# Two attention and gated-MLP layer pairs on one core: the up product copied by ScalarE, and the first chunk planned ahead

## The chip, the core and the metric

The kernel runs on one core of a Trainium2 chip. The engines of that core work side by side, each through its own queue in order: TensorE (PE in the profile; PEld is its weight load) multiplies matrices into PSUM, VectorE (DVE) and ScalarE (ACT) do element work between PSUM and SBUF, GpSimd (POOL) does some set-up, and SyncE (SP) issues the DMA transfers. An engine that needs another's result waits on a semaphore, and everything behind the waiting instruction waits with it. The metric is the device time of one execution in microseconds, taken as the median of several.

## The reference

The input x has 2048 tokens of 576 numbers in bfloat16. Four layers follow each other, attention and MLP in turn, and the same weights serve both pairs:

```python
x = x + A(layernorm(x))   # attention
x = x + B(layernorm(x))   # gated MLP
x = x + A(layernorm(x))
x = x + B(layernorm(x))

# A: 32 heads of 18; token s sees the 8 tokens s, s-2, ..., s-14
qkv = x @ wqkv
logits = einsum("bhsd,bhswd->bhsw", q, kg) * scale    # masked before token 0
o = einsum("bhsw,bhswd->bhsd", softmax(logits), vg)
A = o @ wo

# B: F = 4608, no activation function
h = (x @ w_gate) * (x @ w_up)
B = h @ w_down
```

## The kernel before

**Chunks.** The tokens are worked through in 17 pieces called chunks (j = 0 to 16). Each goes through one attention layer and the MLP behind it. The first two chunks have 128 tokens (nst = 1), the other fifteen 256 (nst = 2). The first eight token tiles go through both layer pairs, and then the other eight. All weights of the MLP but w_down stay in SBUF; w_down is read again for every chunk, two blocks of 128 rows at a time, into seven places.

**The MLP.** The 36 blocks of 128 hidden features are made in units of 512 columns in PSUM: 9 units in a chunk of 128 tokens, 18 in one of 256. A unit has one bank for the gate product (pg) and one for the up product (pu). In the wide chunks the contraction is cut in two halves of 64 rows that run side by side in the array (`quarter`, L947): a unit's first half, then that of its neighbour, then the two second halves. Between the halves stands a one-element copy by ScalarE (`fence`, L493), which makes the second half's matmuls wait for the first's. When a unit's products are complete, `evac` (L960) empties it: ScalarE copies the gate product to SBUF as bfloat16 (L964), and VectorE multiplies the up product, read from PSUM, with it (L965). The result h goes to one of six places, and the unit's banks are free when VectorE is done. A third of the units makes a phase (nph = 3); at its end `down` or `down2` multiplies the phase's h with w_down, in the wide chunks also in two halves (L1021, L1022), and VectorE adds the sums to x (L992, L1001).

**Attention.** `head` (L409) normalises: statistics on VectorE (L417, L418, or in halves L421, L423), the inverse deviation on ScalarE (L432, L433), the factor nmr on VectorE (L437), the normalised rows on ScalarE (L443, L445, L448). The transposed rows come from TensorE in the first chunks (L467, L469, copied out at L474, L476, L479), and from DMA transposes later (L460). `project` (L539) multiplies with wqkv (L549), and the copies out of PSUM are L631, L633, L643, L660 and L667. The scores are products of q with shifted k on VectorE (L704, L727), partly summed there (L708 to L713) and summed over the head by TensorE (L719); then come the maximum (L745), the difference (L749), the exponential (L753), the sum (L757) and its reciprocal (L762). The weights must then stand on all partitions of a head: in the first chunks by a matmul called spread (L781) and copies, later by a round trip through DRAM (L791, L794). The eight products with shifted v are L811. They are added up by VectorE (L833), except in the very first chunk, called fast, where TensorE adds them: `gather` (L813) multiplies each with the identity into the same banks (L815, L816), and VectorE divides at the end (L838, L841). In that chunk the eight products alternate between two places in SBUF, prod0 and prod1. The output projection is L855 or L876, its residual sum L846.

**The start.** The columns of wqkv are permuted after loading (`perm`, L347, copies at L358): five row blocks, for each the query, key and value parts of 512 columns and the tails. VectorE and ScalarE share the query and key parts; the value parts, wq2, are all ScalarE's (VP, L24). TensorE runs matmuls without use (L1138) where the plan sees it idle at the start.

**The order of the work.** Nothing is left to chance in the order: every operation is entered into a `Plan` with an engine, a cost in nanoseconds, what it reads and writes, a priority and a rank. The rank is -1 for urgent work (`due=True`: the work of `evac` and `fence`), the chunk's number for attention, 60 for the MLP, 0.5 for the permutations. `Plan.run` takes the operation that could start first by these costs, and emits the instructions in that order. Before it takes an operation of rank over 0, it looks whether the same engine has one of lower rank that would become ready before the first would end: for rank 0 (the first chunk) within GUARD of that end, for urgent work up to SLACK earlier. The order holds for DMA issues too. The semaphores between the engines follow from the data; the plan's times only give the order.

Of the kernel before, what the change touches and what calls it, by code (L numbers as in the profile page):

```python
# [10 lines left out]
ACT = mybir.ActivationFunctionType  # L11
ALU = mybir.AluOpType
# [4 lines left out]
class Op:  # L17
    __slots__ = ("eng", "cost", "fn", "deps", "order", "succ", "n", "prio", "idx", "hold", "free",
                 "lat", "margin", "ready", "end", "nbytes", "use", "pair", "need", "rank", "late", "half")
# [7 lines left out]
IDLE = (2000, 300)  # L27
GUARD = {"DVE": 300, "ACT": 300, "PE": 600, "POOL": 0, "SP": 0}
# [4 lines left out]
class Plan:  # L33
# [13 lines left out]
    def op(self, eng, cost, fn, r=(), w=(), prio=1, after=None, hold=None, free=None, margin=0, nbytes=0, use=None,  # L47
           pair=None, need=None, due=False, late=0, half=False):
        o = Op()
        o.rank, o.late, o.half = -1 if due else self.rank, late, half  # L50
# [32 lines left out]

    def run(self, slots):
        clock = {e: 0.0 for e in self.LAT}
# [5 lines left out]
        while cand:  # L91
            best = None
            urgent = {}
            for o in cand:
                t = 0.0
                for p in o.deps:
                    e = p.ready if p.eng != o.eng else p.end
                    if e > t:
                        t = e
                t += o.margin  # L100
                if o.hold is not None:
                    f = free[o.hold]
                    if not f:
                        continue
                    t = max(t, min(f)[0] + o.margin)
                if o.pair is not None:
                    if len(free["unit"]) < len(o.pair):
                        continue
                    t = max(t, min(free["unit"])[0] + o.margin)
                if o.need is not None:  # L110
                    t = max(t, o.need["at"])
                t = max(t, clock[o.eng])
                key = (t, o.prio, o.idx)
                if best is None or key < best[0]:
                    best = (key, o)
                urgent.setdefault(o.eng, []).append((key, o))
            assert best is not None, "the plan is stuck"
            o = best[1]
            if o.rank > 0:
                end = best[0][0] + o.cost  # L120
                ahead = [(c[1].rank, c[0], c[1]) for c in urgent[o.eng] if c[1].rank < o.rank and c[1].rank < LOOK[o.eng]
                         and c[0][0] < end + GUARD[o.eng] * (c[1].rank == 0) - SLACK[o.eng] * (c[1].rank < 0)
                         and c[0][0] < best[0][0] + IDLE[min(max(c[1].rank, 0), 1)]]
                if ahead:
                    best = min(ahead, key=lambda c: c[:2])[1:]
# [28 lines left out]
            if o.free is not None:  # L154
                u = o.use
                u["last"] = max(u.get("last", 0.0), o.ready)
                u["left"] = u.get("left", 1) - 1
                if u["left"] == 0:
                    free[o.free].append((u["last"], u["slot"]))
            o.fn()  # L160
            done += 1
            for s in o.succ:
                s.n -= 1
                if s.n == 0:
                    cand.append(s)
# [4 lines left out]
def kernel(  # L170
# [162 lines left out]

    def setup_b():
# [11 lines left out]
        for k in range(KT):  # L346
            def perm(eng, cost, key, t3, rk, k=k):  # L347
# [10 lines left out]
                op(eng, cost, lambda: fn(dst, src), r=rk, w=[key], prio=2 + (t3 in (2, 4)))  # L358
# [29 lines left out]
        op("ACT", 0, lambda: None, r=[f"wq{t}_{k}" for t in (2, 4) for k in range(KT)], w=["s11", "s12", "ab"])  # L388
# [20 lines left out]
    def head(src, keys, nst, dst, key, prio, ab, on_pe, mg, c0=0, halves=False, parts="nt", xr=()):  # L409
# [3 lines left out]
        for i in range(nst if "n" in parts else 0):  # L413
# [5 lines left out]
            if halves:  # L419
                for a in range(2):  # L420
                    op("DVE", 400, lambda a=a, i=i: nc.vector.bn_stats(out=st[:, ia + i, a, :], in_=src(i)[:, a * HD:(a + 1) * HD]),  # L421
                       r=[f"{keys[i]}h{a}"], w=[f"st{ab}{ia + i}{a}"], prio=prio)
                op("DVE", 210, lambda i=i: nc.vector.bn_aggr(out=mv[:, ia + i, :], in_=st[:, ia + i]),  # L423
# [91 lines left out]
    def attention(j, la, t0, nst):  # L515
# [23 lines left out]
        def project(tag, au, bu, tl, ea, eb, dkeys):  # L539
# [5 lines left out]
            wk = [f"wq{t}_{k}" for t in tw for k in range(KT)]  # L545
# [41 lines left out]
            elif fast:  # L587
                o = None
                for part in (0, 1):
                    u, parts, ts = (ua, au + bu[4:5], (0, 1, 3)) if part == 0 else (ub, bu[:4] + bu[5:], (2, 4))  # L590
                    key = (ka, kb)[part]
                    for k in range(KT):
                        def fn(k=k, part=part):
# [7 lines left out]
                            else:  # L601
# [4 lines left out]
                               r=xk + [f"wq{t}_{k}" for t in ts], w=[key], prio=0, **kw)  # L606
# [91 lines left out]
        for p_ in range(W // 2):  # L698
# [25 lines left out]
            pk, sk = f"prod{p_ % 2}", f"s1{p_}"  # L724
            if nst == 2:
                for e in range(2):
                    op("DVE", 70 + 2.6 * n, lambda p_=p_, e=e: nc.vector.tensor_tensor(  # L727
                        late["prod"][p_ % 2][:, e, :, 0:n], qT[:, :, 0:n], kT[:, :, HALO - DIL * (2 * p_ + 1 - e):HALO - DIL * (2 * p_ + 1 - e) + n], op=ALU.mult),
                       r=qk, w=[pk], prio=prio)
            else:  # L730
                op("DVE", 70 + 5.2 * n, l1, r=qk, w=[pk], prio=prio)
            if fast:
                kw = b1.take() if p_ == 0 else dict(w=[b1.key])
                op("PE", 20 * 20, lambda p_=p_: esel(p_, lambda: [late["prod"][p_ % 2][:, :, k, :] for k in range(KT)]),
                   r=["sel", pk, "cap", "ident"], prio=0, **kw)
            else:
                op("DVE", 82 + 2.02 * n, l2, r=[pk], w=[pk], prio=prio)
                op("DVE", 276 + 2.02 * n, l3, r=[pk], w=[sk], prio=prio)
# [65 lines left out]
        for i_ in range(W):  # L804
# [3 lines left out]
            def pv(i_=i_, o0=o0, to_o=to_o):  # L808
# [4 lines left out]
            def gather(i_=i_):  # L813
                pr = late["prod"][i_ % 2][:, 0]
                nc.tensor.matmul(bo[0]()[:, 0:KF * n], lhsT=ident[:], rhs=pr[:, 0:KF, 0:n], start=(i_ == 0), stop=(i_ == W - 1))  # L815
                nc.tensor.matmul(bo[1]()[:, 0:n], lhsT=ident[:], rhs=pr[:, KF, 0:n], start=(i_ == 0), stop=(i_ == W - 1))  # L816
            op("DVE", 70 + 2.63 * n, pv, r=vk + abk, w=["oT"] if to_o else [f"prod{i_ % 2}"], prio=prio)
            if fast:
                if i_ == 0:
                    ob0 = op("PE", 0, lambda: None, w=[bo[1].key], prio=0, hold=bo[1].pool, use=bo[1].use)  # L820
                    op("PE", 330, gather, r=["prod0", "ident"], w=[bo[0].key, bo[1].key], prio=0, hold=bo[0].pool, use=bo[0].use)
# [8 lines left out]
                else:  # L830
                    op("PE", 330, gather, r=[f"prod{i_ % 2}", "ident"], w=[bo[0].key, bo[1].key], prio=0)
            elif i_:
                op("DVE", 70 + 2.63 * n, lambda i_=i_: nc.vector.tensor_tensor(oT[:, :, 0:n], oT[:, :, 0:n], late["prod"][i_ % 2][:, 0, :, 0:n],  # L833
                                                                        op=ALU.add), r=[f"prod{i_ % 2}"], w=["oT"], prio=prio)
# [71 lines left out]
    def glu(j, t0, nst, last):  # L906
# [53 lines left out]
        def evac(u):  # L960
# [3 lines left out]
            op("ACT", 490, lambda: nc.scalar.copy(g_sb[gs][:, 0:ul], pg[use["slot"]][:, 0:ul]), r=[f"wg_{j}_{u}"], w=[f"g{gs}"], prio=0, due=True)  # L964
            op("DVE", 605, lambda: nc.vector.tensor_tensor(hb[hs][:, 0:ul], pu[use["slot"]][:, 0:ul], g_sb[gs][:, 0:ul], op=ALU.mult),  # L965
# [158 lines left out]
    for j, (l, t0, nst) in enumerate(seq):  # L1124
# [8 lines left out]
        if j == 0:  # L1133
            op("PE", 0, lambda: None, w=list(pool_keys["boot"]), free="unit", use={"slot": NB - 1})
# [6 lines left out]
    with tc.manual_schedule():  # L1141
        nc.vector.memset(g_sb[1][:], 0.0)
        pl.run({**{k: len(v) for k, v in banks.items()}, "unit": NB - 1})
# [28 lines left out]
```

## Time and profile before

| | |
|---|---|
| median of 3 runs | 1048.43 us (1048.34 to 1051.18) |
| the profiled execution | 1051.13 us, its span 1049.3 us |
| TensorE busy | 1033.9 us, 99% |
| VectorE busy | 783.3 us, 75% |
| ScalarE busy | 409.6 us, 39% |
| GpSimd busy | 8.5 us, 1% |
| HBM | 113 GB/s over the span |
| granted TensorE clock | 1.0 |

A line of a group of instructions gives the line of the code, the engine, the operation, what it writes and reads, shapes and count; then the time in which the group was busy, the mean duration in nanoseconds, and the idle time of the engine just before, with what ended it. Neighbours on an engine overlap a little: two instructions of 586 ns that follow each other take less than twice that. A line of a timeline gives the start, the duration, the engine and the instruction, with "x4" where several were merged. A line of waits names who waited, for whom, the sum in microseconds, how often, and the longest.

### The profile page before, as it was taken

How to read it: one execution, taken by the hardware profiler on the slowest of the kernel's cores; microseconds unless marked ns; L12 is line 12 of the kernel's file. 1: busy time of each engine (PE TensorE's matmuls, PEld its weight loads, DVE VectorE, ACT ScalarE, POOL GpSimd, SP SyncE). 2: the span in 40 equal slices, each digit the busy share in tenths (PEclk: the TensorE clock that was granted, in tenths of full speed). 3: DMA queues.
4: the chain of work that ended last, by engine and by line, in shares of the span. 5: the costliest groups of instructions: out<-in, count | busy, mean ns of one | idle time of the engine just before them, and what ended most of it. 6: DMA issues, size and time to landing. Idle time of an engine off the chain costs nothing.

```text
span 1049.3 us, 40035 instructions
## 1 busy us (share of the span) xinstructions
PE 1033.9 (99%) x17898; PEld 827.8 (79%) x17909; DVE 783.3 (75%) x1446; ACT 409.6 (39%) x1105; POOL 8.5 (1%) x33
## 2 busy tenths in 40 slices
PE   7999999999999999999999999999999999999998
PEld 3888778789798887878887777877887788777776
DVE  7698978898899879797989573675878748833233
ACT  6643533243434553333434223434344252232231
POOL 3000000000000000000000000000000000000000
PEclk9999999999999999999999999999999999999999
DMA  8967333443425433335352625233252334343332
GB/s 253 328 209 217 88 101 110 144 108 94 99 91 134 137 76 125 107 110 164 89 130 76 179 72 132 93 103 95 88 157 82 99 91 127 117 133 98 116 103 70
DMA packets 144541, 129.67 MB, mean 124 GB/s; under 512 B 43440, under 2 KB 143728, under 8 KB 144368
## 3 DMA queue, kind: packets, MB, share of 16 engines
q1 hardware_dynamic: 144368, 127.10, 42.7%
q8 instruction: 140, 2.29, 0.9%
q14 instruction: 33, 0.27, 0.1%
HBM read 114.02 MB, written 4.19 MB: 113 GB/s over the span
## 4 chain that ended last, share of the span: by engine, by line
PE 84%; DVE 10%; DMA 3%; issue 1%; ACT 1%; SPq 1%; DVEq 0%; ACTq 0%
PE pg L953 16%; PE pu L953 16%; PE pu L1021 6%; PE acct L953 6%; PE pa L953 6%; PE pa L1021 5%; PE pg L1021 5%; PE acct L1021 4%; PE pg L549 3%; PE pu L549 3%; DVE scr L811 2%; PE pg L855 2%; DVE oT L833 2%; PE pu L929 2%; PE pg L929 1%; DMA scr<-a_dram 1%
## 5 line engine op out<-in xcount | busy, mean ns | idle before, releaser
L953 PEld LDWEIGHTS <-wg 64*128 64x128 bf16 x4320 | 393.7, 94 | 30.5 <-issue 1.7
L953 PE MATMUL pg<-xnT_B,wg 64*128 64x256 bf16 x3200 | 412.3, 269 | 1.6 <-ACT xnT_B L479 1.1
L953 PEld LDWEIGHTS <-wu 64*128 64x128 bf16 x4320 | 392.4, 94 | 25.7 <-issue 1.7
L953 PE MATMUL pu<-xnT_B,wu 64*128 64x256 bf16 x3200 | 411.4, 269 | 0.1
L1021 PEld LDWEIGHTS <-h 64*128 64x128 bf16 x2112 | 122.6, 94 | 102.5 <-DVE h L965 1.0
L1022 PE MATMUL pg<-wd,h 64*128 64x64 bf16 x1008 | 190.5, 189 | 0.0
L1022 PE MATMUL pu<-wd,h 64*128 64x64 bf16 x1008 | 190.5, 189 | 0.0
L965 DVE TENSOR_TENSOR h<-pu,g_sb 128x512 bf16<-128x512 f32 x218 | 147.1, 686 | 49.8 <-ACT g_sb L964 49.2
L493 ACT COPY tok<-pu 1x1 f32<-1x1 f32 x291 | 42.8, 147 | 322.0 <-PE pu L953 214.0
L964 ACT CAST g_sb<-pg 128x512 bf16<-128x512 f32 x218 | 126.9, 586 | 103.8 <-PE pg L953 85.0
L953 PE MATMUL acct<-xnT_B,wg 64*128 64x256 bf16 x1120 | 152.7, 269 | 0.0
L953 PE MATMUL pa<-xnT_B,wu 64*128 64x256 bf16 x1120 | 152.4, 269 | 0.2
L1021 PE MATMUL pu<-wd,h 64*128 64x512 bf16 x576 | 149.5, 377 | 0.4 <-ACT tok L493 0.3
L1021 PE MATMUL pg<-wd,h 64*128 64x512 bf16 x576 | 149.3, 377 | 0.2 <-DVE h L965 0.2
L1021 PE MATMUL pa<-wd,h 64*128 64x512 bf16 x480 | 123.8, 377 | 0.0
L1021 PE MATMUL acct<-wd,h 64*128 64x512 bf16 x480 | 123.7, 377 | 0.0
L1022 PEld LDWEIGHTS <-h 64*128 64x128 bf16 x2112 | 121.6, 95 | 1.2 <-issue 0.4
L549 PEld LDWEIGHTS <-wqkv 64*128 64x128 bf16 (+1 forms) x2030 | 102.8, 94 | 15.8 <-issue 3.5
L727 DVE TENSOR_TENSOR scr<-qT,kv 128x1280 bf16<-128x1280 bf16 x112 | 88.5, 816 | 25.7 <-ACT kv L633 25.7
L953 PE MATMUL pg<-xnT_B,wgu_t 64*128 64x256 bf16 x400 | 107.6, 269 | 0.0
L953 PE MATMUL pu<-xnT_B,wgu_t 64*128 64x256 bf16 x400 | 107.6, 269 | 0.0
L549 PE MATMUL pg<-xnT_A,wqkv 64*128 64x256 bf16 (+2 forms) x863 | 100.0, 265 | 1.1 <-DVE xf L1001 0.8
(172 smaller groups left out, 1497.3 us busy)
## 6 DMA issues: line engine op xcount, KB each, us to landing
wd<-in_B_w_down_dram SPq DMA_DIRECT2D x306, 288.0 KB, 4.5
scr<-a_dram SPq DMA_DIRECT2D x56, 128.0 KB, 2.7
wg<-in_B_w_gate_dram SPq DMA_DIRECT2D x6, 768.0 KB, 9.5
wu<-in_B_w_up_dram SPq DMA_DIRECT2D x6, 768.0 KB, 11.2
xb<-in_A_x_dram SPq DMA_DIRECT2D x7, 288.0 KB, 2.9
out_dram<-xf SPq DMA_DIRECT2D x14, 144.0 KB, 3.3
a_dram<-scr SPq DMA_DIRECT2D x14, 128.0 KB, 2.0
scr<-in_A_wqkv_dram SPq DMA_DIRECT2D x4, 288.0 KB, 5.2
```

The costliest lines, as they stand in the source:

```text
L493: box["at"] = nc.scalar.copy(tok[0:1, :], src())
L549: return nc.tensor.matmul(bank(p_, u)[0:m, e * n:(e + 1) * n], lhsT=wqkv[r_, k, w0:w0 + m], rhs=xnT_A[r_, k, c0:c0 + n], start=start, stop ...
L727: op("DVE", 70 + 2.6 * n, lambda p_=p_, e=e: nc.vector.tensor_tensor(late["prod"][p_ % 2][:, e, :, 0:n], qT[:, :, 0:n], kT[:, :, HALO - DI ...
L811: nc.vector.tensor_tensor(js(dst), js(vT[:, :, o0:o0 + n]), abw, op=ALU.mult)
L833: op("DVE", 70 + 2.63 * n, lambda i_=i_: nc.vector.tensor_tensor(oT[:, :, 0:n], oT[:, :, 0:n], late["prod"][i_ % 2][:, 0, :, 0:n], op=ALU. ...
L855: return nc.tensor.matmul(bank(hh, us[i])[:, 0:HD], lhsT=oT[rows, t, i * P:(i + 1) * P], rhs=wo_p[rows, t, hh * HD:(hh + 1) * HD], start=( ...
L929: nc.tensor.matmul(pt[:, e * n:(e + 1) * n], lhsT=w_[:, k, ft * P:(ft + 1) * P], rhs=xT[:, k, 0:n], start=(first and k == 0 and e == 0), s ...
L953: return nc.tensor.matmul(ps[:, e * n:(e + 1) * n], lhsT=w_, rhs=xT[rows, k, 0:n], start=(first and e == 0 and k == 0), stop=(not first an ...
L964: op("ACT", 490, lambda: nc.scalar.copy(g_sb[gs][:, 0:ul], pg[use["slot"]][:, 0:ul]), r=[f"wg_{j}_{u}"], w=[f"g{gs}"], prio=0, due=True)
L965: op("DVE", 605, lambda: nc.vector.tensor_tensor(hb[hs][:, 0:ul], pu[use["slot"]][:, 0:ul], g_sb[gs][:, 0:ul], op=ALU.mult), r=[f"wu_{j}_{ ...
L1021: return [lambda: nc.tensor.matmul((pg, pu)[i][use["slot"]][:], lhsT=lhs, rhs=wt[rows, e % 2, 0:512], start=first, stop=fin, skip_group_ch ...
L1022: lambda: nc.tensor.matmul((pg, pu)[i][tl["slot"]][:, 0:TL], lhsT=lhs, rhs=wt[rows, e % 2, 512:D], start=first, stop=fin, skip_group_check ...
```

## The change

In `evac`, for every chunk but the first, ScalarE now copies the up product too, from PSUM into the place of h, after the gate product. This copy frees the unit's banks. VectorE then multiplies h with the gate in SBUF, in place, with both operands in bfloat16.

`Plan.ahead` is new. Before the real plan it runs a plan of the first chunk and the set-up alone, emitting nothing, and notes for each operation of rank 0 when it starts there (`res`). In the real plan an operation of rank 1 or more is put behind such a reserved stretch if it would reach into it by more than TOL; if the first chunk runs late, the reservations shift with it. GUARD becomes smaller, and the look for work of lower rank is left out for operations that cost under 100 ns.

Each value permutation is cut into two halves, and the plan gives each half to VectorE or ScalarE, whichever would be done first (`alts`). The first chunk's products with v go to four places: prod0 and prod1 are each treated as two. The bank of the output sums' last part is taken only when the spread weights are there. For chunks whose transposes are TensorE's, the statistics are entered as three operations, not one.

```diff
-GUARD = {"DVE": 300, "ACT": 300, "PE": 600, "POOL": 0, "SP": 0}
+GUARD = {"DVE": 50, "ACT": 50, "PE": 100, "POOL": 0, "SP": 0}
+TOL = {"DVE": 100, "ACT": 100, "PE": 100, "POOL": 1e9, "SP": 1e9}
...
+    def ahead(self, slots, last):
+        every, emit = self.ops, self.fill
+        ops = [o for o in every if o.idx < last and o.rank < 1]
...
+        self.ops, self.fill = ops, None
+        self.run(slots)
+        self.ops, self.fill = every, emit
...
+        for o in ops:
+            if o.rank == 0 and o.cost and o.eng != "SP":
+                o.res = o.end - o.cost
...
+                if o.alts:
+                    o.eng = min(o.alts, key=lambda e: (clock[e] + o.alts[e], e))
+                    o.cost, o.lat = o.alts[o.eng], self.LAT[o.eng]
...
+                if o.rank >= 1 and o.cost:
+                    for b0, c0, _, _ in book[o.eng]:
+                        if t + o.cost > b0 + shift + TOL[o.eng] and t < b0 + shift + c0:
+                            t = b0 + shift + c0
...
-            if o.rank > 0:
+            if o.rank > 0 and o.cost >= 100:
...
+            if o.res is not None:
+                book[o.eng].remove((o.res, o.cost, o.idx, o))
+                shift = max(0.0, t - o.res)
...
+                        box["o"] = op("ACT", 565, half, r=rk, w=[f"{key}{'ab'[hf]}"], prio=3, alts={"DVE": 320, "ACT": 565})
...
+            if on_pe:
+                for a in range(2):
+                    op("DVE", 400, lambda a=a, i=i: nc.vector.bn_stats(out=st[:, ia + i, a, :], in_=src(i)[:, a * HD:(a + 1) * HD]),
...
-                dst = oT[:, :, 0:n] if to_o else late["prod"][i_ % 2][:, 0, :, 0:n]
+                dst = oT[:, :, 0:n] if to_o else late["prod"][i_ % 2][:, pb, :, 0:n]
...
-                    ob0 = op("PE", 0, lambda: None, w=[bo[1].key], prio=0, hold=bo[1].pool, use=bo[1].use)
+                    ob0 = op("PE", 0, lambda: None, r=abk, w=[bo[1].key], prio=0, hold=bo[1].pool, use=bo[1].use)
...
+            if j > 0:
+                op("ACT", 490, lambda: nc.scalar.copy(hb[hs][:, 0:ul], pu[use["slot"]][:, 0:ul]), r=[f"wu_{j}_{u}"], w=[f"h{hs}"], prio=0, due=True,
+                   free="unit", use=use)
+                op("DVE", 350, lambda: nc.vector.tensor_tensor(hb[hs][:, 0:ul], hb[hs][:, 0:ul], g_sb[gs][:, 0:ul], op=ALU.mult),
+                   r=[f"g{gs}", f"h{hs}"], w=[f"h{hs}"], prio=0, due=True)
+                return hs
             op("DVE", 605, lambda: nc.vector.tensor_tensor(hb[hs][:, 0:ul], pu[use["slot"]][:, 0:ul], g_sb[gs][:, 0:ul], op=ALU.mult),
...
+        room = {**{k: len(v) for k, v in banks.items()}, "unit": NB - 1}
+        pl.ahead(room, boot)
+        pl.run(room)
```

More of the change, by code (lines that the diff above doesn't have):

```diff
@@ L18 @@
     __slots__ = ("eng", "cost", "fn", "deps", "order", "succ", "n", "prio", "idx", "hold", "free",
-                 "lat", "margin", "ready", "end", "nbytes", "use", "pair", "need", "rank", "late", "half")
+                 "lat", "margin", "ready", "end", "nbytes", "use", "pair", "need", "rank", "late", "half", "res", "alts")
 POOLQ = False
@@ L357, in perm, with half @@
                 pl.rank = 0.5
-                op(eng, cost, lambda: fn(dst, src), r=rk, w=[key], prio=2 + (t3 in (2, 4)))
+                if t3 == 2:
+                    for hf in range(2):
+                        box = {}
+                        def half(hf=hf, box=box):
+                            f = {"DVE": nc.vector.tensor_copy, "ACT": nc.scalar.copy}[box["o"].eng]
+                            f(dst[:, 8 * hf:8 * hf + 8], src[:, 8 * hf:8 * hf + 8])
+                        box["o"] = op("ACT", 565, half, r=rk, w=[f"{key}{'ab'[hf]}"], prio=3, alts={"DVE": 320, "ACT": 565})
+                else:
+                    op(eng, cost, lambda: fn(dst, src), r=rk, w=[key], prio=2 + (t3 == 4))
                 pl.rank = 0
@@ L387, in setup_b @@
         op("DVE", 0, lambda: None, r=[f"wq{t}_{k}" for t in (0, 1, 3) for k in range(KT)], w=["prod0", "prod1", "s10", "Lt"])
[L388 removed]
+        op("ACT", 0, lambda: None, r=[x for t in (2, 4) for k in range(KT) for x in wqk(t, k)], w=["s11", "s12", "ab"])
     def setup_wo():
```

63 lines of the change are left out of this document (44 added, 19 removed).

## The prediction

> **What bounds the kernel now.** I read the page first: its busy line, then its costliest groups.
>
> ```profile
> span 1049.3 us, 40035 instructions
> ...
> PE 1033.9 (99%) x17898; PEld 827.8 (79%) x17909; DVE 783.3 (75%) x1446; ACT 409.6 (39%) x1105; POOL 8.5 (1%) x33
> ...
> L965 DVE TENSOR_TENSOR h<-pu,g_sb 128x512 bf16<-128x512 f32 x218 | 147.1, 686 | 49.8 <-ACT g_sb L964 49.2
> ...
> L964 ACT CAST g_sb<-pg 128x512 bf16<-128x512 f32 x218 | 126.9, 586 | 103.8 <-PE pg L953 85.0
> ```
>
> TensorE is busy almost everywhere, so shorter work on VectorE counts only where TensorE waits for it. The two groups are the instructions that the change touches most. Where TensorE is not busy I took from the busy times by stretch (columns: length, then PE, PEld, DVE, ACT, POOL):
>
> ```profile
> 0.00:33.00 33.00, 25.43 (x311) 15.79 (x316) 25.55 (x67) 21.45 (x41) 8.51 (x33) 1.00 0.94 270
> 33.00:100.00 67.00, 66.50 (x1053) 53.54 (x1057) 55.63 (x111) 34.36 (x78) 0.00 (x0) 1.00 0.81 242
> 100.00:150.00 50.00, 47.50 (x813) 38.78 (x814) 42.89 (x77) 21.55 (x57) 0.00 (x0) 1.00 0.42 124
> 150.00:600.00 450.00, 448.28 (x7909) 365.29 (x7906) 388.04 (x707) 181.17 (x507) 0.00 (x0) 1.00 0.42 113
> 600.00:1049.30 449.30, 446.20 (x7828) 354.44 (x7824) 271.23 (x487) 151.12 (x423) 0.00 (x0) 1.00 0.37 106
> ```
>
> TensorE idles 7.6 us before 33 (and much of its work there is filler, L1138, 8.3 us in all), 0.5 to 100, 2.5 to 150, 1.7 to 600, and 3.1 after, nearly all of that the last slice (21.21 busy of 24.3). So 4.7 us in the middle is all that any relief of VectorE can give, and the rest is the start. From 150 to 600 VectorE is 86% busy, later 60%, where TensorE does not wait. TensorE's waits between 100 and 150 are these:
>
> ```profile
> PE pg L953 <- ACT xnT_B L479: 1.1, 1, 1.1
> PE pg L549 <- DVE xf L1001: 0.8, 1, 0.8
> PE pu L549 <- DVE xf L1001: 0.5, 1, 0.5
> ```
>
> The start I read from the timelines. The first gated-unit matmul (L929) starts at 32.87; before it one chain runs through the first chunk, and these VectorE rows lie on it or in its way:
>
> ```profile
> 10.62 0.82 DVE L417 BATCH_NORM_STATS2 st<-xb 128x6 f32<-128x288 bf16 x2
> 11.47 0.21 DVE L418 BATCH_NORM_AGGREGATE mv<-st 128x2 f32<-128x12 f32 x1
> 11.59 0.96 DVE L631 CAST kv<-pu 128x512 bf16<-128x512 f32 x2
> 12.66 3.03 DVE L704 TENSOR_TENSOR scr<-qT,kv 128x1280 bf16<-128x1280 bf16 x4
> 15.61 0.81 DVE L417 BATCH_NORM_STATS2 st<-xb 128x6 f32<-128x288 bf16 x2
> 16.45 0.21 DVE L418 BATCH_NORM_AGGREGATE mv<-st 128x2 f32<-128x12 f32 x1
> 16.69 0.42 DVE L745 TENSOR_REDUCE mx<-pu 128x32 f32<-128x256 f32 x1
> ```
>
> L417 at 10.62 and 15.61 belongs to later chunks; the first chunk's k copy (L631) and row maximum (L745) stand behind it.
>
> **The change, part by part.** The sum is made against the profiled execution: 1051.13 us, of which 1049.3 is span and 1.8 lies around it. The median of the runs is 1048.43, 2.7 below that execution, so I carry the difference over to the median and not the sum itself.
>
> **Units.** Of 288 units (218 + 70 multiplies at L965) the first chunk's 9 keep the old form; 279 change. Each gains a ScalarE copy of 512 elements out of PSUM, priced by L964: 586 ns, and 0.48 to 0.49 when two follow each other (36.65, 1.05 us for two). Added: 279 x 0.49 = 137 us, so ScalarE goes from 410 to about 547 us, 52%. The multiply falls from 686 ns (0.61 between neighbours) to that of a bf16 multiply in SBUF, which the trace does not show. Its bounds are the 512-wide SBUF rows: L713, bf16 throughout, 425; and L760, one float32 operand, 691. I take 425, since the types are L713's: 0.34 between neighbours by the same overlap of some 80 ns, so VectorE loses 279 x 0.27 = 75 us and ends near 710. At 691 it would lose nothing. None of either is on the path as such; what counts is who waits. Behind the new copy on ScalarE stand the next unit's gate copy and the one-element copies L493 that let the second half of a unit start. I laid the new copies into one steady phase of the timeline: gate copies at 642.16 and 643.03, L493 at 644.12, next gate copies at 646.09 and 646.96. With up copies between them the four run 642.16 to 644.22, so L493 slips by about 0.1 us; the matmuls that it releases stand behind another quarter of a unit, till about 645.2, so 0.9 us of cover remains. The last multiply of a phase would end near 648.6 instead of 648.27, and its down-projection matmuls come at about 249 (10 steps of 0.25 us after 646.7, so 649.2): 0.6 us of cover, before 0.9. The PSUM place comes free about 0.1 us earlier. In steady state this part is worth nothing either way.
>
> **Less VectorE work where TensorE waits.** In 100 to 150, the wait of 1.1 us ends with the third chunk's transposed activations, whose residual sum stands behind VectorE work that was full (19.6 of 20 us busy from 90 to 110); chunk 1's nine units free 9 x 0.27 = 2.4 us there, so I take 1.0 of it as gone. The waits of 1.3 us on L1001 come from a VectorE queue that stood 3.87 us for the round trip of the attention weights through DRAM (up to 138.24), and then did five value products ahead of the sums; shorter multiplies do not shorten that round trip, so I take 0.7. Of the 1.7 us to 600 I take half, 0.8. Against this I set 0.7 us of new waits on ScalarE: its slower answers cost 1.1 us once already, and 0.1 us in seven places is of that size. Sum of the middle: -1.8, bounds -4.2 (all waits go) to +2 (none goes, new ones come).
>
> **The first chunk.** (a) Keeping L417/L418 of chunk 1 out of the way: the key projection's last matmul ends at 11.03, the copy starts at 11.59, and on ScalarE q's copy starts at 11.37 behind a value permutation; 0.5. (b) The last score matmul ends at 16.07, the maximum starts at 16.69 behind 15.61's statistics; 0.55. (c) The second spread of the weights (L781) waits till 19.18 for the bank that the first holds, since the other bank of the two is already held for the output sums; the new order takes that bank later. VectorE was busy till 19.47 anyway, and its copy starts at 19.66; 0.2. (d) The eight value products run from 20.44 to 24.49, 4.05 us. Two places alternate, and the third product starts (21.45) only when the first gather has ended. The first two, unhindered, are 0.41 apart: 7 x 0.41 + 0.49 = 3.36, so four places give 0.7. (e) Residual, normalisation: L417 at 26.31 stands before the residual (0.2), and at 29.21 L417 on VectorE and at 29.74 L443 on ScalarE stand before the normalised row, which starts at 30.49 and could at 30.02 (0.45). Together 0.5 + 0.55 + 0.2 + 0.7 + 0.65 = 2.6 us.
>
> Given back: the displaced work must go somewhere. Chunk 1's projections (27.46 to 30.74) fill a gap that TensorE has anyway between the output projection's end at 27.63 and 32.87; the gap gets 0.65 shorter and its other pieces nearly fill it, so I return 0.2. Sharing out the value permutations: on ScalarE 512 elements take 1.13 us (L358) and they occupy it from 10.36 to 17.05 with little between; halves that VectorE takes cost it about 0.32 each (128 elements 0.28, 512 elements 0.63). If three went there onto the chain that is +1.0, if they fall into VectorE's own gaps (15.6 to 16.1, 17.6 to 18.1) nothing, and ScalarE is free earlier; I take 0, because the values are needed only at 20.44. The smaller statistics pieces cost no time and fit such gaps. The DMA queue of SyncE is given its order by the same plan, but no transfer is added; the last weights of the first phase landed at 30.4 and their matmuls (L940) come 2.8 us after the first L929, so they would hold it up only if it started before 27.6. Left: 2.4 us, bounds -3.0 to 0.
>
> Sum: -2.4 - 1.8 = -4.2, so 1051.1 becomes 1046.9 in a like execution and the median 1044.2.
>
> [...] The rows above say that a unit costs ScalarE 0.49 us more and VectorE 0.27 less: 0.22 us more engine time per unit, 61 us over all. That the engine which gets it stood idle 61% of the span is why I don't charge it. [...]
>
> **Rivals.** One: the first chunk does not get earlier for the whole, because what is pushed aside (statistics, projections of chunks 1 and 2) is missing later, and TensorE stands between 33 and 60 instead; for it: VectorE is nearly full from 55 on and the later weights land as late as 59.7; against: TensorE idled only 0.5 us from 33 to 100. Then -0.4 for the start and -1.3 for the middle: 1046.7, no change that can be told.
>
> Two: ScalarE becomes the gate. It holds four copies per pair of units, 1.96 us in a pair's 3.9, and its other work (0.87 and 0.43 us of L443 and L445) can't be broken. At each phase's end the last h has 0.6 us of cover. There are 15 wide chunks x 3 phases = 45 such places; if ScalarE were late by one L443 at each, 0.87 - 0.6 = 0.27 us x 45 = 12 us, less the start's 2.4: 1058. It decides from (4.2 + 3.1) / 45 = 0.16 us per phase on. For it: the plan allows an urgent ScalarE operation to be delayed by 300 ns; against: ScalarE waits for TensorE, not the other way, in the whole list (L493 214 us).
>
> Three: the multiply runs at L760's 691 ns. Then VectorE gets no relief, each h is 0.6 us later and the cover is used up: the middle is +1, the sum -1.4, 1047.0.
>
> **How the numbers follow.** A measurement of this kernel tells 0.3% (3.1 us) from no change; its runs spread 1048.3 to 1051.2. Forecast 0.55, on its own 1041.5 to 1046; rival one 0.22; rival two 0.15, more of it near 1053 than at 1058; rival three 0.08. Faster by over 0.3% (under 1045.3): most of the forecast, with a few hundredths where all waits go; 0.56. Same: rivals one and three and the forecast's upper edge, 0.28. Slower: rival two, 0.16. The range goes from 1041.0 (both lower bounds, -7.2, at 1041.2) to 1052.5, into rival two.
>
> **What would show it.** The first L929 near 30.5; no L417 of a later chunk between the key projection and L745; value products 0.41 apart; the changed multiply near 425 ns, ScalarE near 547 busy, VectorE near 705; TensorE's idle time in 100 to 150 about 1 us. Wrong: TensorE waits named after ScalarE's copies that add up to more than 2 us, the first L929 no earlier than 32, or idle time growing between 33 and 100.

## The result and the profile after

The changed kernel takes 1053.23 us (median of 22 runs, 1051.0 to 1055.85), the kernel before 1050.45 in the same comparison (22 runs, 1048.34 to 1054.79). The ratio is 1.0028, with a 95% interval of 1.0019 to 1.0037: 2.8 us slower, where 4.2 us faster had been forecast. The forecast of 1044.2 was set on the median of three runs, 1048.43; 22 runs of the kernel before put that 2.0 us higher, so of the 9.0 us by which it missed, 7.0 are the change's. The two profiled executions show only 1.0 of these 2.8 us (1051.13 before, 1052.09 after), because that of before lies 0.7 above its median and that of after 1.1 below. So the profiles tell where time went; how much, the medians tell.

The page of the changed kernel, its busy line and the groups of the multiply and of the two copies:

```profile
span 1049.8 us, 40397 instructions
...
PE 1034.2 (99%) x17906; PEld 805.3 (77%) x17906; DVE 713.0 (68%) x1450; ACT 527.8 (50%) x1385; POOL 8.3 (1%) x33
...
L1028 DVE TENSOR_TENSOR h<-h,g_sb 128x512 bf16<-128x512 bf16 x279 | 116.1, 419 | 149.9 <-ACT h L1026 148.1
...
L1024 ACT CAST g_sb<-pg 128x512 bf16<-128x512 f32 x208 | 123.3, 595 | 78.8 <-PE pg L1013 62.8
...
L1026 ACT CAST h<-pu 128x512 bf16<-128x512 f32 x199 | 120.2, 604 | 0.0
```

The multiply (now L1028) takes 419 ns instead of 686, VectorE is busy 70 us less and ScalarE 118 us more. The parts did what they were to do. The busy times by stretch of the changed kernel (columns as before):

```profile
0.00:33.00 33.00, 25.36 (x305) 15.48 (x305) 26.51 (x71) 20.16 (x42) 8.35 (x33) 0.95 0.96 290
33.00:100.00 67.00, 67.00 (x1065) 53.74 (x1063) 54.42 (x112) 37.13 (x84) 0.00 (x0) 1.00 0.77 233
100.00:150.00 50.00, 50.00 (x867) 40.35 (x866) 43.45 (x82) 28.13 (x74) 0.00 (x0) 1.00 0.41 123
150.00:600.00 450.00, 446.40 (x7871) 350.53 (x7869) 363.26 (x715) 232.58 (x627) 0.00 (x0) 1.00 0.42 114
600.00:1049.80 449.80, 445.47 (x7814) 345.16 (x7810) 225.31 (x473) 209.79 (x561) 0.00 (x0) 1.00 0.37 105
```

TensorE's idle time, length less busy, by stretch: 7.6 us to 33 as before (with a mean granted clock of 0.95 for 1.00); nothing from 33 to 150, where it was 3.0; 3.6 instead of 1.7 from 150 to 600, and 4.3 instead of 3.1 after. What the first stretches gain, the later ones lose. The list of TensorE's waits in the changed kernel names the new ones:

```profile
PE pg L1087 <- DVE h L1028: 2.7, 5, 0.8
PE pu L875 <- DVE scr L871: 2.0, 1, 2.0
...
PE pa L1013 <- ACT tok L550: 0.6, 2, 0.4
```

The down-projection (L1087) waits 2.7 us for h; before it was 0.2 us. In the first chunk the gather (L875) waits 2.0 us for its product. The fence of ScalarE (L550), a one-element copy that the second half of a unit waits for, had been feared; it costs 0.6.

**One place where h is late.** The timeline of the changed kernel from 322 to 329, the rows of three engines brought together in order of time:

```profile
322.31 0.83 DVE L871 TENSOR_TENSOR oT<-kv,scr 128x1280 bf16<-128x1280 bf16 x1 [1.66 <-DMA scr<-a_dram]
323.05 0.76 DVE L1028 TENSOR_TENSOR h<-h,g_sb 128x512 bf16<-128x512 bf16 x2
324.31 0.59 ACT L1026 CAST h<-pu 128x512 bf16<-128x512 f32 x1
325.27 0.62 ACT L1026 CAST h<-pu 128x512 bf16<-128x512 f32 x1
326.92 0.42 DVE L1028 TENSOR_TENSOR h<-h,g_sb 128x512 bf16<-128x512 bf16 x1
327.39 0.39 PE L1087 MATMUL pg<-wd,h 64*128 64x512 bf16 x1 [0.77 <-DVE h L1028]
327.99 0.42 DVE L1028 TENSOR_TENSOR h<-h,g_sb 128x512 bf16<-128x512 bf16 x1
328.46 0.39 PE L1087 MATMUL pg<-wd,h 64*128 64x512 bf16 x1 [0.41 <-DVE h L1028]
```

ScalarE has finished its up copies at 324.90 and 325.89. The multiplies start 2.0 and 2.1 us later, at 326.92 and 327.99: not ScalarE holds them up but the order of VectorE's queue. There the value products (L871, L893) stand before them, and the first of these stood 1.66 us, until 322.31, for the attention weights to come back from DRAM. That is more than the 1.18 us that TensorE then waits. The write had been issued at 314.2 and landed at 317.5; the four reads landed from 319.7 to 322.3; the way out and back took 8.1 us. From 764 to 773 the same picture returns (2.00 us of standing, up copies done some 2 us ahead of their multiplies, then waits of 0.71 and 0.41). The two places make up 2.3 of the 2.7 us.

**The first chunk.** The timeline of the changed kernel at the start, again of three engines:

```profile
12.26 3.03 DVE L761 TENSOR_TENSOR scr<-qT,kv 128x1280 bf16<-128x1280 bf16 x4
15.93 0.42 DVE L802 TENSOR_REDUCE mx<-pu 128x32 f32<-128x256 f32 x1
19.42 3.31 DVE L871 TENSOR_TENSOR scr<-kv,scr 128x640 bf16<-128x640 bf16 x8
19.96 0.38 PE L875 MATMUL pu<-scr,ident 128*128 128x512 bf16 x1 [2.05 <-DVE scr L871]
21.28 0.63 PE L875 MATMUL pu<-scr,ident 128*128 128x512 bf16 x1
24.15 0.76 DVE L898 TENSOR_TENSOR oT<-pu,rzs 128x256 bf16<-128x256 f32 x2 [0.81 <-PE pg L876]
25.20 0.87 ACT L500 ACTIVATE xn<-xb,nmr,rstd 128x576 bf16<-128x576 bf16 x1 [1.30 <-DVE nmr L494]
28.60 0.65 ACT L505 ACTIVATE xn<-xf,nmr,rstd 128x320 bf16<-128x320 f32 x1 [0.23 <-DVE nmr L494]
33.44 1.07 PE L989 MATMUL pg<-xnT_B,wg 128*128 128x128 bf16 x16
```

The chain does come earlier: score products 0.40, the maximum 0.76, the value products 1.0, the normalised row 1.9 us (28.60 for 30.49). But the first gated-unit matmul (L989) starts at 33.44, not at 30.5, and 0.6 us later than before. Two things lie between. TensorE stood idle 2.05 us ahead of the gathers, where the kernel before has filler; after that its gathers, from the fourth on, took 0.63 instead of 0.38 us each, with a granted clock of 0.66 between 20 and 25. And chunk 1's normalised row (L500) comes at 25.20, before at 22.09, since its statistics are now kept out of the way. Its projections, which started at 27.46 as the output projection ended (27.63), now start 1.4 us behind it (27.76 for 26.35). In both kernels all of them stand in TensorE's order ahead of the first gated-unit matmul, 4.96 us of matmuls with the transposes among them; TensorE idles 0.45 us in between before and 0.72 now. The last of chunk 1's projections, before and now:

```profile
31.93 0.61 PE L549 MATMUL pu<-xnT_A,wqkv 128*128 128x128 bf16 x8
32.50 0.61 PE L606 MATMUL pu<-xnT_A,wqkv 128*128 128x128 bf16 x8
```

From the first chunk's normalised row to the first gated-unit matmul it is 4.84 us now and was 2.38: what the chain gains is lost again there.

### The profile page after: what moved, and what is told of

Read it like the earlier page. It is cut to its first block, busy times and chain, and to the rows that moved or that the text cites. A ratio compares the mean times of both kernels' runs of the same rounds, so it can differ in the third digit from the quotient of the medians.

```text
span 1049.8 us, 40397 instructions
## 1 busy us (share of the span) xinstructions
PE 1034.2 (99%) x17906; PEld 805.3 (77%) x17906; DVE 713.0 (68%) x1450; ACT 527.8 (50%) x1385; POOL 8.3 (1%) x33
## 4 chain that ended last, share of the span: by engine, by line
PE 78%; DVE 14%; DMA 4%; ACT 2%; issue 1%; SPq 1%; DVEq 0%
PE pg L1013 15%; PE pu L1013 13%; PE pu L1087 9%; PE pg L1087 7%; PE pa L1013 7%; PE acct L1013 6%; PE pg L606 4%; PE pu L606 3%; DVE scr L784 2%; DVE oT L893 2%; DVE scr L871 2%; PE pu L989 2%; PE pg L989 2%; DMA scr<-a_dram 2%; PE pg L1047 2%; DMA a_dram<-scr 1%
## 5 line engine op out<-in xcount | busy, mean ns | idle before, releaser
L1013 PE MATMUL pu<-xnT_B,wu 64*128 64x256 bf16 x3040 | 392.0, 269 | 0.7 <-DVE xf L1067 0.6
L1087 PE MATMUL pg<-wd,h 64*128 64x512 bf16 x1032 | 267.1, 377 | 3.2 <-DVE h L1028 2.7
L1087 PE MATMUL pu<-wd,h 64*128 64x512 bf16 x1032 | 267.4, 377 | 0.0
L1028 DVE TENSOR_TENSOR h<-h,g_sb 128x512 bf16<-128x512 bf16 x279 | 116.1, 419 | 149.9 <-ACT h L1026 148.1
L1087 PEld LDWEIGHTS <-h 64*128 64x128 bf16 x2112 | 114.9, 94 | 114.6 <-DVE h L1028 6.9
L1013 PE MATMUL pa<-xnT_B,wu 64*128 64x256 bf16 x1280 | 174.2, 269 | 0.6 <-ACT tok L550 0.6
L1013 PE MATMUL acct<-xnT_B,wg 64*128 64x256 bf16 x1280 | 174.1, 269 | 0.0
L1088 PE MATMUL pg<-wd,h 64*128 64x64 bf16 x840 | 158.8, 189 | 0.0
L1088 PE MATMUL pu<-wd,h 64*128 64x64 bf16 x840 | 158.8, 189 | 0.0
L550 ACT COPY tok<-pu 1x1 f32<-1x1 f32 x272 | 39.9, 147 | 232.5 <-PE pu L1013 165.5
L1026 ACT CAST h<-pu 128x512 bf16<-128x512 f32 x199 | 120.2, 604 | 0.0
L606 PE MATMUL pu<-xnT_A,wqkv 64*128 64x256 bf16 (+1 forms) x807 | 95.5, 265 | 0.7 <-DVE xf L1067 0.4
```

The costliest lines, as they stand in the source:

```text
L550: box["at"] = nc.scalar.copy(tok[0:1, :], src())
L606: return nc.tensor.matmul(bank(p_, u)[0:m, e * n:(e + 1) * n], lhsT=wqkv[r_, k, w0:w0 + m], rhs=xnT_A[r_, k, c0:c0 + n], start=start, stop ...
L1013: return nc.tensor.matmul(ps[:, e * n:(e + 1) * n], lhsT=w_, rhs=xT[rows, k, 0:n], start=(first and e == 0 and k == 0), stop=(not first an ...
L1026: op("ACT", 490, lambda: nc.scalar.copy(hb[hs][:, 0:ul], pu[use["slot"]][:, 0:ul]), r=[f"wu_{j}_{u}"], w=[f"h{hs}"], prio=0, due=True, fre ...
L1028: op("DVE", 350, lambda: nc.vector.tensor_tensor(hb[hs][:, 0:ul], hb[hs][:, 0:ul], g_sb[gs][:, 0:ul], op=ALU.mult), r=[f"g{gs}", f"h{hs}"] ...
L1087: return [lambda: nc.tensor.matmul((pg, pu)[i][use["slot"]][:], lhsT=lhs, rhs=wt[rows, e % 2, 0:512], start=first, stop=fin, skip_group_ch ...
```

## The experiments

Each kernel was timed beside the kernel before on the same chip; ratios are to that. The kernel before stood at 1050.4 us beside the first four kernels below, at 1050.11 beside the next three on VectorE's queue (`late` at 3500 and 0, no delay on VectorE) and the control, at 1049.8 beside its own version and the units alone at 3500, no delay on ScalarE and both at once, and at 1050.12 beside the two at 3500 without filler.

**The parts alone.** First `evac` alone in the kernel before, then the start alone, that is the changed kernel with the old `evac`:

```diff
 # units alone, in before
+            if j > 0:
+                op("ACT", 490, lambda: nc.scalar.copy(hb[hs][:, 0:ul], pu[use["slot"]][:, 0:ul]), ...
+                op("DVE", 350, lambda: nc.vector.tensor_tensor(hb[hs][:, 0:ul], hb[hs][:, 0:ul], g_sb[gs][:, 0:ul], op=ALU.mult), ...
+                return hs
 # start alone, in after: the same lines taken out
```

> The kernel before with the units' part alone: ScalarE also copies the up product from the second chunk on, VectorE multiplies in SBUF. Theory A (the loss is ScalarE's and sits in the units: the multiply comes later at the end of each phase, and TensorE waits for h in front of the down-projection, 2.7 us in the changed kernel against 0.2): slower than before by 1 to 3 us. Theory B (the loss is the start's, a TensorE that idles 2.05 us ahead of the first gather and then runs at half rate): the units' part alone gains, 1 to 3 us faster than before, since between 33 and 150 us TensorE idled 3.0 us less in the changed kernel.

> The changed kernel with the units as before: only the first chunk laid out ahead, four places, shared permutations, smaller guards. Theory A: 1 to 3 us faster than before. Theory B: 2 to 4 us slower than before, with matmuls of 0.63 us among the gathers and a granted clock below 1.0 over the first 33 us, as in the changed kernel (0.95).

Units alone: 1052.23 us, ratio 1.0015 (1.0003 to 1.0026), 1.8 us behind. Start alone: 1050.65, ratio 1.0003 (0.9991 to 1.0015), nothing. So the units lose, and the start gains none of its 2.4 us; there both theories missed, the gain of 1 to 3 us and the loss of 2 to 4. Units alone show the same wait for h as the whole change (waits of TensorE, from 100 us on):

```profile
PE pg L1027 <- DVE h L968: 2.9, 5, 1.4
```

**Filler ahead of the gathers.** The plan puts filler where TensorE has a gap since its last entry. An entry without cost (`ob0`) now waits for the weights and sets the plan's clock of TensorE forward, so no gap is seen. Nine filler matmuls written out by hand close it:

```diff
 # in gather(), with the change whole, and with the start alone
+                if i_ == 0:
+                    fill(9)
```

> The changed kernel with nine more matmuls without use in front of the first gather, in the place where TensorE idled from 17.9 to 19.96 us. Theory B: the gathers keep 0.38 us and come 0.40 apart, the last ends near 22.9 instead of 24.15, the granted clock of the first 33 us is 1.0, and the time falls by 1 to 3 us against the changed kernel. Theory A: the time stays within 0.5 us of the changed kernel's.

> The units as before, the start as changed, with the nine matmuls. Theory B: against the start alone 1 to 3 us faster, and about as fast as the kernel before or up to 1.5 us faster. Theory A: as the start alone.

The whole with filler takes 1051.20 us, ratio 1.0011 (0.9998 to 1.0023); the start alone with filler 1049.68, ratio 0.9994 (0.9984 to 1.0004). The granted clock from 20 to 25 is 1.00, and the whole's first gate copy comes 15.81 us after its first gather instead of 16.70. The idle stretch cost 1.0 us with the old units and, across two comparisons, 2.0 with the new. Even so the start is worth only 0.7 us, which its interval doesn't tell from nothing, and the units lose 1.5 between these two kernels.

With filler the first chunk's normalised row does come 2.4 us earlier than in the kernel before, counted from the first score product (15.46 us behind it, for 17.83). The first gated-unit matmul is no earlier by that count (20.29 for 20.21). In each of the twelve profiles with the new start it is 4.83 or 4.84 us from that row to that matmul.

**What h waits for.** Either the round trip through DRAM makes VectorE late, or ScalarE does. The plan counts a transfer as landed at a time worked out from its bytes, 2000 ns, and `late`. I changed `late` of the four reads, and then what delay the plan allows urgent work on VectorE and on ScalarE:

```diff
 # reads of the attention weights, with change and filler: 3500, and 0
-                   r=[f"adr{j % 2}", "ab"], w=[f"ab{g}"], prio=0, nbytes=P * W * sq * 2, late=1200)
+                   r=[f"adr{j % 2}", "ab"], w=[f"ab{g}"], prio=0, nbytes=P * W * sq * 2, late=3500)
 # with change and filler, 1200 kept
-SLACK = {"DVE": 500, "ACT": 300, "PE": 0, "POOL": 0, "SP": 0}
+SLACK = {"DVE": 0, "ACT": 300, "PE": 0, "POOL": 0, "SP": 0}
 # the same for ScalarE
+SLACK = {"DVE": 500, "ACT": 0, "PE": 0, "POOL": 0, "SP": 0}
```

> The changed kernel with the nine matmuls; the plan now expects the attention weights to land from DRAM 2.3 us later (late 3500 for 1200). Only the order changes. Theory R (the units' loss comes from VectorE's queue: value products are planned for a landing that comes up to 2.7 us late, VectorE stands, and the multiplies planned behind them reach TensorE late): the waits of TensorE on the multiply fall from 3.4 us to under 1, VectorE's waits for the landing shrink, and the time falls by 0.5 to 2 us against the same kernel with 1200. Theory D (the plan lets attention work go ahead of an urgent multiply by up to 500 ns): waits and time as with 1200, within 0.5 us.

> The changed kernel with the nine matmuls, and the plan expects the landing 1.2 us earlier (late 0 for 1200): the dose the other way. Theory R: VectorE waits for landings grow from 13.9 us to over 20, the waits on the multiply from 3.4 to over 5 us, and the time grows by 1 to 3 us. Theory D: within 0.7 us.

> The changed kernel with the nine matmuls; urgent work on VectorE is no longer delayed by other work in the plan (SLACK of DVE 0 for 500). Theory D: the waits on the multiply fall from 3.4 us to under 1, and the time falls by 0.5 to 2 us against the same kernel with 500. Theory R: a value product that waits for its landing still stands in front of a multiply, so 2 us of the waits stay; and since attention gets later, the time stays or grows by up to 3 us (the plan's own end moves from 1038.6 to 1042.2).

> The whole change with filler between the first gathers, and the plan no longer allows urgent ScalarE work to be delayed by up to 300 ns (0). If ScalarE's lateness (the prediction's rival two) cost time in the middle, this gains 1 us or more on the same kernel with 300 (1051.2). By the theory that VectorE's queue is what h waits in, it lies within 0.7 us of it.

With `late` at 0, 1200 and 3500 the kernel takes 1062.64 (ratio 1.0125, 1.0105 to 1.0145), 1051.20 and 1047.33 us (0.9969, 0.9958 to 0.9981). No delay for urgent work on VectorE: 1047.73 (0.9977, 0.9968 to 0.9987). No delay on ScalarE: 1050.91 (1.0011, 1.0002 to 1.0021), 0.3 us from 1051.20. So the order on VectorE is worth 3.5 to 3.9 us. At 0 the loss is 11.4 us where 1 to 3 were expected, and not by h alone: in that profile TensorE waits 4.6 us for h, 3.6 for the attention's residual sum (L908) and 3.3 at the fences.

The run without delay on ScalarE settles less than its time says. In its profile TensorE no longer waits for h at all, but instead for ScalarE: 2.7 us at the fences (L550), where it was 0.9, 1.1 for transposed rows (L536) and 0.7 for keys (L690). One kind of wait was exchanged for another, so that ScalarE's delay has no part in the waits for h isn't shown.

With a later landing in the plan the waits of TensorE for h fall from 3.4 us: with `late` at 3500,

```profile
PE pg L1089 <- DVE h L1030: 0.4, 1, 0.4
```

and with no delay on VectorE, a line of VectorE's waits and one of TensorE's, from 100 us on:

```profile
DVE oT L871 <- DMA scr<-a_dram: 31.0, 10, 4.7
PE pg L1089 <- DVE h L1030: 1.0, 1, 1.0
```

The second pair says what matters. VectorE stands 31.0 us for the landing, more than twice the 14.6 of the changed kernel, and TensorE loses little for h, since by the plan nothing less urgent may now delay a multiply. Here the standing as such costs TensorE nothing; it costs when something that TensorE needs is queued behind it. In the kernel before, which stands 33.0 us, that is the residual sums (L1001, 1.3 us of waits) rather than h (0.2).

**Is it the units' loss?** The control: the start with the old units and filler, at 3500.

> The units as before, the start as changed, nine matmuls, and the late landing in the plan: a control. If R holds for the new units alone, this stays within 0.7 us of the same kernel with 1200; if it gains as much as the changed units do, the landing is a fault of the kernel before as well, and no part of the change's loss.

It takes 1046.88 us (0.997, 0.9959 to 0.9981): the old units gain 2.8 us by the same figure, the new ones 3.9. By what was expected of this run, the landing is then a fault of the kernel before too, and what is left for the change is the difference of some 1.1 us. So I took it to the kernel before and to the units alone, on one chip:

> The kernel before with one figure changed: its plan reckons 3500 ns, not 1200, for the landing of the attention weights from DRAM. With the run below it asks whether the units' part (two ScalarE copies, multiply in SBUF) has a cost of its own. Theory (the loss of the units' part is a wait of the multiplies behind a VectorE that stands for the landing): this kernel gains 2 to 3 us on the kernel before, as the one with the new start and the old units did (2.8), so 1047 to 1048.5. Rival (the landing hurts only with something of the change, here the new start): within 1 us of the kernel before.

> The units' part alone with the landing reckoned at 3500 ns. Theory: the units' own cost goes with the waits behind the landing, so this lies within 0.7 us of the kernel before with 3500 (units alone lost 1.8 at 1200), and TensorE waits for h under 1 us in all. Rival (the units cost by themselves: ScalarE's copies, or one more step from product to h): it stays 1.5 to 2 us behind that kernel. Second rival (shorter VectorE work was worth something all along, hidden by the landing): over 0.7 us ahead of it.

The kernel before at 3500: 1047.66 us (0.9976, 0.9968 to 0.9985). Between its two profiled executions VectorE's standing falls from 33.0 to 9.6 us, TensorE's waits for the residual sums L1001 from 1.3 to 0.2, and its idle time from 100 to 600 from 4.2 to 1.9. Units alone at 3500: 1048.09 (0.998, 0.997 to 0.999). The units now lose 0.4 us where they lost 1.8. TensorE's and VectorE's waits of the units alone at 3500, from 100 us on:

```profile
DVE oT L811 <- DMA scr<-a_dram: 2.6, 4, 1.8
PE pg L1027 <- DVE h L968: 0.4, 1, 0.4
```

Two more at 3500, without filler, price the rest: the whole change, and the start with the old units.

> The whole change as it is, without filler, its plan reckoning 3500 ns for the landing. Beside the same with filler (1047.3) it prices TensorE's idle stretch of 2 us at the start. Theory: the stretch and the half clock behind it cost 1 to 1.7 us here, so 1048.3 to 1049. Rival (with the landing reckoned rightly the middle takes it up): within 0.5 us of 1047.3. Second rival (the 2.0 us that filler was worth at 1200 is its full price): 1049.3.

> The start's part with the old units and without filler, landing reckoned at 3500 ns. Beside the same with filler (1046.9) and the kernel before with 3500 (1047.7). Theory: filler is worth 1 us with the old units too, so 1047.6 to 1048.2, and the start's part as it was made gains nothing on the kernel before. Rival (the start gains 0.8 us without filler as well): under 1047.2.

They take 1048.03 us (0.9981, 0.9972 to 0.999) and 1047.73 (0.9978, 0.9968 to 0.9987). Of the four kernels run without filler that have the new start, this last one's profiled execution is the only one with a granted clock of 1.00 from 20 to 25, for 0.66 in the other three:

```profile
19.82 0.38 PE L875 MATMUL pu<-scr,ident 128*128 128x512 bf16 x1 [2.05 <-DVE scr L871]
...
21.43 0.38 PE L875 MATMUL pu<-scr,ident 128*128 128x512 bf16 x1
```

Medians in us, by what the kernel has and by `late` (within a column the kernels before of the comparisons differ by 0.3 us at most):

| | 1200 | 3500 |
|---|---|---|
| before | 1050.4 | 1047.66 |
| units | 1052.23 | 1048.09 |
| start | 1050.65 | 1047.73 |
| units and start (the change) | 1053.23 | 1048.03 |
| start, filler | 1049.68 | 1046.88 |
| units, start, filler | 1051.20 | 1047.33 |

Of the change's 2.8 us, 0.4 is left in the second column. The units cost 1.5 to 2.6 in the first and 0.3 to 0.45 in the second; differences of that last size are at the edge of what these runs tell. The start without filler gains nothing in either, and beside the new units at 1200 it loses 1.0; filler is worth 0.7 to 0.85 at 3500. Why it was worth 2.0 with the new units at 1200, twice what it is elsewhere, stays open.

**Both at once.** No delay for urgent work on VectorE and 3500 together, in the whole change with filler:

> The whole change, filler between the first gathers, landing reckoned at 3500 ns and no delay of urgent VectorE work allowed (0 for 500). Each of the two took 3.5 to 3.9 us alone. Theory (both remove the same waits of h in VectorE's queue): they do not add, 1046 to 1047.5. Rival (two separate losses): under 1045.

1046.90 us (0.9973, 0.9962 to 0.9983): 0.4 and 0.8 us less than either alone by the medians, not told apart from them by the ratios, and far from the 7 us that two separate losses would have added up to. In the main they remove the same waits. Each of the kernels at 3500 beats both of the case's kernels, the plainest by one figure in the kernel before. The lowest ratio is that of the whole change with filler and 3500, 0.9969; its interval overlaps that of all the others at 3500.

## Why the prediction was wrong

**Sizes of the units' part: right.** 425 ns were taken for the multiply and 419 measured; VectorE was to end near 710 and is at 713; ScalarE at 527.8 for 547, since the copies add 118 us to it (120 in the units alone) and not 137. Rival three (691 ns) is out.

**"In steady state this part is worth nothing either way": the step that failed for the middle.** The cover of 0.6 us was worked out in one phase in which VectorE did units alone, and lateness was looked for on ScalarE. It holds there. But in the phases in which VectorE stands for the attention weights and then does value products, multiplies queue behind these, 2 us in the place shown. The prediction had seen such a standing (3.87 us, up to 138.24) and charged it to one reader only, the residual sums L1001. It asked what shorter multiplies free, not what else is in that queue.

**The middle's terms.** The waits between 100 and 150 were to lose 1.7 of 2.5 us; all 2.5 went. "Of the 1.7 us to 600 I take half" had the wrong sign: 3.6. "0.7 us of new waits on ScalarE": 0.6 at the fence, right, and missing beside it are 2.7 us of waits for h. The sum of -1.8 is +1.8 in the run of the units alone, of which 1.4 hangs on the landing. The other 0.4 I can only place: between the two kernels at 3500 idle time falls from 1.2 to 0.05 us in 100 to 150 and rises from 0.7 to 2.0 up to 600, with no single wait over 0.6 us behind it.

**The start, -2.4: "given back" is the step that failed.** Steps (a) to (e) happened nearly as worked out: 0.40 for 0.5, 0.76 for the 1.05 of (a) and (b) by the maximum, products 0.40 apart for 0.41, and 1.9 of the 2.6 us by the normalised row. With filler, at a granted clock of 1.00 from 20 to 25, (b) to (e) bring 2.4 us for their 2.1. (d) fell short: the products end 1.8 us earlier, the sum that they feed only 1.3 (24.15 for 25.43), since the gathers behind them ran at a granted clock of 0.50 (21.5 to 24.0), 0.53 us apart. Filler under (c) was overlooked: the later entry of the bank takes it away and opens 2.05 us. The larger mistake is "I return 0.2". The gap that the prediction wanted to shorten was full: it took chunk 1's projections to end at 30.74, but twelve more matmuls of them and transposes follow ahead of the first L929, and of the 5.41 us from 27.46 to 32.87 TensorE idled only 0.45. And the pieces that were pushed aside are themselves the head of chunk 1's chain; its row comes 3.1 us later, so its projections start late, and the first L989 stands behind them. From the first chunk's row to that matmul 2.46 us are given back (4.84 for 2.38), not 0.2. This is read from the traces; no run put those projections behind the matmul. With filler at most 0.7 to 0.8 us of the 2.4 is left, without it nothing.

**The rivals.** Rival one named the outcome of the start rightly (earlier for the chunk, not for the whole), but put the idle time between 33 and 60, where there is none; it lies before 33. Rival two is the nearest to the middle: an h late at a phase's end. But in the places shown its ScalarE isn't late, and the urgent delay whose removal saved time was VectorE's 500 ns and not ScalarE's 300: taking each to 0 moved 3.5 and 0.3 us, the second by exchanging waits. No rival had the queue behind the DRAM round trip. The time lies 0.7 us above the range; a loss of 2.8 us on the base of 1048.43 would have lain inside it, on rival two's side and for another reason.

**The engine time that was weighed.** A unit's 686 ns on VectorE became 419 there and 604 more on ScalarE. At 3500 that pays nothing, or -0.4 us.

## What to carry to other kernels

Before an operation is made to depend on one more engine, list what stands ahead of it in each of its queues, in the busiest phase and not in a quiet one, and above all what there waits for a transfer. A plan made in advance holds only if its landing times hold: vary them first, since here one such figure was worth 2.7 us to the kernel before and made most of the units' loss. When work is moved out of a chain's way, find whose chain it heads, count what else the bounding engine must do before it can use the gain, and see that the filler of the place it leaves survives.

## What was unexpected of the hardware

The same gap was followed by different clocks. In the changed kernel, in the start alone and in the whole at 3500 without filler, TensorE idled 2.05 us ahead of the gathers, most of these ran at 0.55 to 0.63 us for 0.38, and the granted clock from 20 to 25 was 0.66; in the start at 3500 without filler the same 2.05 us were followed by gathers of 0.38 us and a clock of 1.00. In half microseconds the granted clock of the changed kernel is 1.00 up to 21.0, 0.54 to 21.5, 0.50 to 24.0, 0.54 to 24.5 and 1.00 behind that: the first three gathers, from 19.96 on, still take 0.38 us. In the start alone the first one already takes 0.59.

Lower clocks show in other places too: 0.97 from 100 to 150 in the two kernels with no delay on VectorE, where TensorE's longest wait from 100 us on was 1.6 us (L1015, for transposed rows), and 0.95 to 33 in the units alone at 3500, where no wait over 1.2 us is listed. So the length of a gap doesn't tell alone, and what the fall of the clock depends on is not shown by these runs.

The mean clock of each run, which doesn't tell where in the kernel it fell, gives a price. Of the 55 runs of the four kernels with the gap ten have 1.0 and the others 0.998 or less; within each kernel the others take 1.2 to 1.9 us more by the median, and most of all in the changed kernel, where two runs have 1.0.

Most of the spread of the runs goes with the landing. In one comparison the kernel before runs from 1047.62 to 1053.55 us (34 runs), and with 3500 from 1047.28 to 1048.07 (12 runs); the whole with filler from 1049.73 to 1056.64, and from 1047.06 to 1048.53. The landing isn't its only condition: without delay on ScalarE the whole with filler runs only from 1050.22 to 1051.68, at 1200.
